# Causal convolution into a token-mixing MLP: one band matrix, halo rows in the loads, weights cast by their loads, and a written job list

## The chip, the cores and the metric

The kernel runs on one core of one Trainium2 chip. The metric is the device time of one execution in microseconds (us), as the median of several runs. Engines are named as the profile names them: PE (TensorE), PEld (its weight loads), DVE (VectorE), ACT (ScalarE), POOL (GpSimd) and SP (SyncE).

## The reference

The input x has 8 batches of 4224 tokens with 192 channels. A causal convolution of 7 taps, with softmaxed weights for each of 8 heads of 24 channels, gives y. Then an MLP mixes tokens through a 64-wide inner space.

```python
w = softmax(weight)                                  # 8 heads, 7 taps
y[b, s, h] = sum_k w[h, k] * x_pad[b, s + k, h]      # x_pad: 6 zero rows in front
wq, wk = y @ w_q, y @ w_k                            # 192 -> 64
W_tok = (wq @ wk.T) / sqrt(64)
out = relu(W_tok @ y) @ w_out                        # 192 -> 192
```

Since nothing nonlinear stands between the two products, W_tok @ y is wq @ (wk.T @ y), and wk.T @ y is w_k.T @ (y.T @ y). The kernel computes the small matrix G = y.T @ y once per batch.

## The kernel before

Everything is a list of operations for five engines, made by a planner in Python when the program is built. Each engine runs its list in order, and each operation waits on semaphores for what it needs. An engine whose next operation waits stands still, whatever is behind it.

**Tiling.** A batch has two halves of 2112 tokens, each cut into 18 chunks of 122 tokens. A chunk is loaded with the 6 rows ahead of it, so it fills 128 partitions; the last chunk has 38 tokens. `XW` holds five batches of x in bf16 (`NX = 5`).

**The stages of a batch.**

- Y (L512 for batch 0, L543 after): the convolution as a matmul with a band matrix for each head. All chunks use `BAND`; the last chunk of a half uses `BANDL`, so a head's last group takes two matmuls. The result goes from PSUM to `Y` (L955, ACT or DVE).
- D: copies 64 columns of `Y` beside the others, so that G can be made from 128-wide windows. For batches 2 and later it runs on POOL.
- T (L953): a transpose on DVE into `YB`. Q (L608): w_q times y, in four row groups and two column groups of PE, for each half of the chunks. It takes four PSUM banks.
- G (L637): six matmuls of 64 columns for each of 18 chunks, all into one PSUM bank. GEV copies G out, TR (L663, L664) transposes a part of it, MM (L677) multiplies by w_k, and the result lands in `M_SB`. No Z of a batch can start before all of its G.
- Z (L713): M times q, 13 jobs a batch, with a relu on the way out (L958 ACT, L959 DVE).
- O (L756, L758): z times w_out, 9 jobs a batch. The result goes to a ring of 8 buffers, `OUT` (`o_sb`), and from there to HBM by SP.

**Loads.** POOL issues the loads of x, which cast f32 to bf16 on the way. Batch 0 comes in eight groups in the order of use. Each further batch comes in two parts: `first` loads chunk 0 of the first half in two pieces without its six halo rows (those are zeroed once), `rows` loads the other chunks, `last` the short ones (L284). Batches 1 to 4 are issued at the start, and D of batch b issues batch b + 4. The loads of w_k and w_out go through SP in f32 into `WST`, and ten jobs W on ACT and DVE cast them. The cast of w_q is on ACT.

**The order.** The planner keeps streams of jobs (Q, W, GEV, TR and MM, O, Z, D, T, Y, G). At each step it takes the job that a model of the engines calls ready, and among several the one with the lowest key, a due time worked out from `KEYS`. It also puts dummy matmuls on PE (L966) where it expects PE to wait early in the run. The evacuation of each job goes to ACT or DVE, whichever the model has free first.

## Time and profile before

| | us |
|---|---|
| median of 13 runs | 161.24 (160.08 to 163.04) |
| the profiled execution | 161.61 |
| its span | 159.5 |
| PE busy in it | 144.1 |
| ACT busy | 129.0 |
| DVE busy | 116.5 |
| POOL busy | 62.2 |

The span is what the profile covers of one execution; the remaining 2.1 us of that execution lie outside it. Line numbers such as L543 are those of the kernel before. A helper records every evacuation, so all of them have L955, L958, L959, L960 or L961, and they are told apart by the tile that they write. Matmuls are pipelined and their ends are modelled, so the distance from one start to the next tells more than the duration of one; some matmul records are missing from the trace.

### The profile page before, as it was taken

To read this page: it belongs to the slowest core of one execution; us is meant where nothing else is said; L and a number is where in the kernel's file an instruction comes from. 1 tells how busy PE (TensorE), PEld (TensorE's weight loads), DVE (VectorE), ACT (ScalarE), POOL (GpSimd) and SP (SyncE) were. 2 spreads that over 40 slices of the span, in tenths; PEclk is the share of its full clock that TensorE was granted. 3 is DMA by queue.
4 is the path that set the end of the run, shared out by engine and by line. 5 is a ranking of instruction groups with operands and counts; after the bars stand their busy time and mean duration, and the time that the engine had idled before them with its cause. 6 is when DMAs were issued, how large, how long until landed. Compare 5 with 4: busy or idle time off the path is not lost.

```text
span 159.5 us, 5869 instructions
## 1 busy us (share of the span) xinstructions
PE 144.1 (90%) x2553; PEld 109.7 (69%) x2584; DVE 116.5 (73%) x233; ACT 129.0 (81%) x225; POOL 62.2 (39%) x83
## 2 busy tenths in 40 slices
PE   5898858999997999999999999999899999999930
PEld 4897753777775677766776787687667777776720
DVE  6758556998748788869778887997679839656700
ACT  8644638999876999799789887978698989799960
POOL 7999999899990755022002020202011020000000
PEclk9999999999999999999999999999999999999995
DMA  3999999999999999999999999999996454669997
GB/s 47 181 168 205 191 191 192 191 190 265 215 254 317 295 199 273 330 264 297 286 292 289 295 290 241 276 339 295 263 318 235 180 218 176 246 259 375 360 384 253
DMA packets 48281, 40.44 MB, mean 254 GB/s; under 512 B 38144, under 2 KB 40320, under 8 KB 48256
## 3 DMA queue, kind: packets, MB, share of 16 engines
q0 software_dynamic: 36784, 13.63, 71.9%
q1 hardware_dynamic: 11472, 26.45, 46.0%
q8 instruction: 20, 0.33, 0.8%
q14 instruction: 5, 0.04, 0.1%
HBM read 27.73 MB, written 25.95 MB: 337 GB/s over the span
## 4 chain that ended last, share of the span: by engine, by line
PE 75%; DMA 6%; ACT 5%; POOL 4%; issue 3%; DVE 3%; ACTq 0%; POOLq 0%
PE ps L637 16%; PE ps L756 13%; PE ps L543 12%; PE ps L758 12%; PE ps L608 9%; PE ps L713 9%; DMA xw<-in_x_dram 6%; POOL xw L268 3%; ACT y L955 2%; ACT o_sb L955 1%; DVE yb L953 1%; PE ps L677 1%; ACT qt L955 1%; DVE zt L959 1%; PE ps L966 1%
## 5 line engine op out<-in xcount | busy, mean ns | idle before, releaser
L955 ACT COPY o_sb<-ps 128x768 f32<-128x768 f32 (+1 forms) x63 | 47.2, 778 | 4.6 <-PE ps L758 3.4
L955 ACT CAST y<-ps 128x864 bf16<-128x864 f32 (+4 forms) x52 | 40.9, 812 | 6.5 <-PE ps L512 5.4
L756 PE MATMUL ps<-wo,zt 128*128 128x192 bf16 x256 | 42.6, 248 | 0.4 <-DVE m_sb L961 0.2
L758 PE MATMUL ps<-wo,zt 128*128 128x384 bf16 x128 | 41.7, 326 | 0.0
L268 POOL DMA_DIRECT2D xw<-in_x_dram x51 | 40.8, 816 | 1.5 <-POOLq L1101 0.8
L955 POOL COPY y<-y 128x1152 bf16<-128x1152 bf16 x12 | 13.9, 1156 | 67.4 <-ACT y L955 53.7
L637 PEld LDWEIGHTS ps<-y 128*128 128x128 bf16 x864 | 32.5, 98 | 8.4 <-ACT y L955 0.6
L637 PE MATMUL ps<-y 128*128 128x64 bf16 x864 | 35.8, 193 | 1.5 <-ACT y L955 0.4
L959 DVE TENSOR_SCALAR zt<-ps 128x512 bf16<-128x512 f32 x47 | 31.2, 683 | 8.0 <-PE ps L713 5.7
L953 DVE STREAM_TRANSPOSE yb<-y 128x576 int32<-128x576 int32 x48 | 33.6, 748 | 0.3 <-ACT y L955 0.2
L756 PEld LDWEIGHTS ps<-wo,zt 128*128 128x128 bf16 x256 | 25.5, 115 | 9.4 <-ACT o_sb L955 1.3
L543 PE MATMUL ps<-xw,band 128*128 128x432 bf16 (+1 forms) x112 | 28.5, 336 | 0.7 <-ACT m_sb L960 0.3
L958 ACT ACTIVATE zt<-ps 128x512 bf16<-128x512 f32 x49 | 28.7, 632 | 0.0
L955 DVE CAST y<-ps 128x864 bf16<-128x864 f32 (+2 forms) x20 | 19.3, 964 | 8.4 <-PE ps L543 5.4
L713 PE MATMUL ps<-qt,m_sb 128*128 128x512 bf16 x65 | 21.8, 380 | 0.3
L955 ACT CAST qt<-ps 128x576 bf16<-128x576 f32 (+2 forms) x21 | 11.7, 583 | 9.3 <-PE ps L608 9.3
L955 DVE CAST qt<-ps 128x234 bf16<-128x234 f32 (+1 forms) x27 | 10.3, 419 | 9.3 <-PE ps L608 9.3
L608 PE MATMUL ps<-yb,wq 32*64 32x288 bf16 x768 | 15.7, 284 | 1.5 <-issue 1.2
L543 PEld LDWEIGHTS ps<-xw,band 128*128 128x128 bf16 x112 | 9.8, 97 | 7.2 <-ACT m_sb L960 0.7
L758 PEld LDWEIGHTS ps<-wo,zt 128*128 128x128 bf16 x128 | 14.5, 113 | 0.0
L713 PEld LDWEIGHTS ps<-qt,m_sb 128*128 128x128 bf16 x96 | 8.8, 97 | 5.7 <-ACT y L955 0.9
L608 PEld LDWEIGHTS ps<-yb,wq 32*64 32x64 bf16 x768 | 10.5, 102 | 2.9 <-issue 1.9
(78 smaller groups left out, 117.0 us busy)
## 6 DMA issues: line engine op xcount, KB each, us to landing
out_dram<-o_sb SPq DMA_DIRECT2D x31, 768.0 KB, 7.3
xw<-in_x_dram POOLq DMA_DIRECT2D x21, 384.0 KB, 27.2
xw<-in_x_dram POOLq DMA_DIRECT2D x7, 432.0 KB, 26.4
xw<-in_x_dram POOLq DMA_DIRECT2D x4, 240.0 KB, 5.6
out_dram<-o_sb SPq DMA_DIRECT2D x16, 48.0 KB, 5.5
out_dram<-o_sb SPq DMA_DIRECT2D x2, 384.0 KB, 3.2
xw<-in_x_dram POOLq DMA_DIRECT2D x8, 42.0 KB, 13.5
xw<-in_x_dram POOLq DMA_DIRECT2D x1, 288.0 KB, 6.2
```

What stands on the lines that cost most here:

```text
L268: return e.dma_start(XW[lo:hi, b % NX, half, c : c + n, :], bass.AP(x_t, at, [[D, hi - lo], [CW * D, n], [1, D]]),)
L543: last = e.matmul(o.rearrange("p (c h d) -> p h c d", h=2, d=GRP), band_[:, h, :], rhs, start=True, stop=True, skip_group_check=True,)
L608: last = e.matmul(PS[64 * h : 64 * h + 64, bk + i, 0:288], WQ[r, j, :], rhs, start=j == 0, stop=j == 5, skip_group_check=True)
L637: last = e.matmul(PS[:, 7, 64 * k : 64 * k + 64], y[:, 64 * k : 64 * k + 128], y[:, 64 * k : 64 * k + 64], start=c + h + k == 0, stop=c == ...
L677: last = e.matmul(PS[:, bk, 64 * k : 64 * k + 64], WK[:, w], src, start=j == 0, stop=j > 2, skip_group_check=True)
L713: return e.matmul(PS[:, bk, :], m[:, parts[k] : parts[k] + 128], q, start=True, stop=True)
L756: e.matmul(o[:, 192 * h : 192 * h + 192], z[:, h, cols], WO1[:, :], start=h == 0, stop=False, **kw)
L758: last = e.matmul(o[:, 0:384], z[:, 2, cols], WO2[:, :], start=False, stop=True, **kw)
L953: return e.transpose(o, i)
L955: return e.copy(o, i) if eng == "act" else e.tensor_copy(o, i)
L958: return e.activation(o, i, AF.Relu)
L959: return e.tensor_scalar(o, i, 0.0, None, op0=ALU.max)
```

## The change

`BANDL` goes: all chunks use `BAND`, and G of the last chunk reads only its 38 valid rows. Batches 1 and later load chunk 0 together with the others, halo rows included, and a new job H zeroes the six rows on DVE once the load is there. Two groups of batch 0 come through SP in f32, into the idle `OUT` buffers, and are cast by ACT and DVE. w_k and w_out are loaded by POOL with the cast in the load, after batch 0; five small copies (the two jobs W) make the variants of the weights. The cast of w_q and two clears move to POOL. Batch 1 comes in four parts, batch 0 in fewer and wider Y jobs. D of batch b issues the load of batch b + 3, and D may go to DVE where POOL is late. The dummy matmuls get wider and fewer. The loop over keys is replaced by `ORDER`, a string with one letter for each job (E is GEV, M is TR and MM in turn, h sets banks aside for a coming Q); the model still decides who evacuates.

```diff
+ORDER = (
+    "YYDYYYDYDGDGGGYDGYYGDGTYTYDhYGhGTGDGGhGGHTGQYDGGWGTEMYMTYYYDZYZGGGTQYZGDGWGGDZZZ"
+    "YOZOOGGGGhGGZTTHGYQGGGYYGYZDEZTYYZGZMGTGDTYGTYZTMGGGGOGOOGGHZQTGGYZGOYZOZZGYDZGY"
+    "TGGZOZZOEYTTOGGYZGQGGYGTZDYZGHMhOGGZQYTGMTGYTTYOZOGOGZZGTZOYOOGZZOGZGDYGEQTGZZMG"
+    "GhQOGZGYYTZOOGHGZYTOGGZMDYGGGYGZGYYOZGZGOZZGDGEOTZQGZMZGGTOYYOGTOZYGDYZZGGhMOGGT"
+    "QHOGZGZTZOGZYOGGZZZYYZGOGYTTOTZOGZGhOEDQZGOYOGTGZTGGMYYOZOGGMZYZODGTOOGHZZGGYZOh"
+    "GGGYThQGZZGZQZTOGYGEZYOOZZZOMYDGYMGYGGZGTZOOTZZZGTGGTYDTGOGOGGQZZZGGOTTZTGZOQZGGO"
+    "QGOGOEMZZZOMOOZZZOZZZZOOOZZZOOZZZOZOOOO"
+)
...
-    BANDL = sbuf("bandl", [128, H, 128], BF16)
-    WST = sbuf("wst", [128, 4, D], F32)
-    WARM = sbuf("warm", [128, 128], BF16)
+    WARM = sbuf("warm", [128, 512], BF16)
...
+        ((0,), 6, 11, EIGHT), ((1,), 5, 10, EIGHT), ((0,), 11, 18, FOURS), ((1,), 10, 14, EIGHT),
         ((1,), 14, 18, FOURS),
-    ]] + [[((0, 1), 0, 9, PAIRS), ((0, 1), 9, 18, PAIRS)]] * (B - 1)
+    ], [
+        ((0,), 0, 9, FOURS), ((1,), 0, 9, FOURS), ((0,), 9, 18, FOURS), ((1,), 9, 18, FOURS),
+    ]] + [[((0, 1), 0, 9, PAIRS), ((0, 1), 9, 18, PAIRS)]] * (B - 2)
...
+    staged = [OUT[:, g, :, :].rearrange("p h c -> p (h c)")[:, 0 : 5 * D] for g in range(2)]
+    for g in range(2):
+        half, c, _, _ = GROUPS[0][g]
+        P.dma(
+            "sp",
...
+                bass.AP(x_t, at, [[D, 128], [CW * D, 5], [1, D]]),
+            ),
+            xg[0][g],
+        )
...
-    rows(0, 0, 1, 0, 128, 5, xg[0][0], ())
+    rows(0, 0, 6, 0, 128, 5, xg[0][3], ())
     bits = pool(lambda e: e.iota(BITS[:, :], [[1, H]], base=127, channel_multiplier=-1))
-    rows(0, 1, 0, 0, 128, 5, xg[0][1], ())
     first(0, xg[0][2], z_first)
-    rows(0, 0, 6, 0, 128, 5, xg[0][3], ())
     rows(0, 1, 5, 0, 128, 5, xg[0][4], ())
...
-    warm(16, [z_warm])
+    warm(4, [z_warm])
...
+    x_cast = act(lambda e: e.copy(fine[0], staged[0]), [xg[0][0]])
...
-    wqs = [act(lambda e: e.copy(WQ[:, :, :], WSQ[:, :, :]), [wl[0]])]
-
-    short = [dve(lambda e: e.tensor_copy(BANDL[0:64, :, 0:LAST], BAND[0:64, :, 0:LAST]),
-                 [*band, z_bandl])]
...
-        if part == 0:
-            first(b, xg[b][0], old)
-            rows(b, 0, 1, 0, 128, 8, xg[b][0], old)
-            rows(b, 1, 0, 0, 128, 9, xg[b][0], old)
+        if b == 1:
+            half, c = part % 2, 9 * (part // 2)
+            rows(b, half, c, 0, 128, 9 - part // 2, xg[b][part], old)
         else:
-            rows(b, 0, 9, 0, 128, 8, xg[b][1], old)
-            rows(b, 1, 9, 0, 128, 8, xg[b][1], old)
-            last(b, xg[b][1], old)
...
+            for half in range(2):
+                rows(b, half, 9 * part, 0, 128, 9 - part, xg[b][part], old)
+        if part == (2 if b == 1 else 1):
+            last(b, xg[b][part], old)
...
+    wload(WK[:, 0], wk_t, 0, DH, wl[1], 2)
+    wload(WK[:, 1], wk_t, 64, DH, wl[1], 2)
+    wload(WK[0:64, 2], wk_t, 128, DH, wl[1], 2)
+    wload(WK[64:128, 2], wk_t, 0, DH, wl[1], 2)
     load(1, 0)
     load(1, 1)
+    wq = [pool(lambda e: e.tensor_copy(WQ[:, :, :], WSQ[:, :, :]), [wl[0]], 0.55)]
+    z_wk = pool(lambda e: e.memset(WK[:, 3:6], 0.0))
+    load(1, 2)
+    z_m = pool(lambda e: e.memset(M_SB[:, :, :], 0.0), (), 0.85)
...
+    load(1, 3)
+    load(2, 0)
+    wload(WO1[:, :], wo_t, 0, D, wl[2])
+    wload(WO2S[0:64, :], wo_t, 128, D, wl[2])
+    wload(WO2S[64:128, :], wo_t, 128, D, wl[2])
+    z_wo2 = pool(lambda e: e.memset(WO2[:, :], 0.0))
+    load(2, 1)
...
-                for band_, a0, a1 in parts(c0, c1):
-                    rhs = XW[:, b % NX, :, a0:a1, GRP * h : GRP * h + GRP]
...
+                rhs = XW[:, b % NX, :, c0:c1, GRP * h : GRP * h + GRP]
+                last = e.matmul(
+                    PS[:, k + j, 0 : 48 * n].rearrange("p (c h d) -> p h c d", h=2, d=GRP),
+                    BAND[:, h, :], rhs, start=True, stop=True,
+                )
...
+    def job_halo(b):
+        return Job(
+            ("H", b), 0, None, [], groups=[xg[b][0]],
+            evacs=[(lambda bk: [(XW[0:6, b % NX, 0, 0, :], None)], ("H", b), 96, "zero")],
         )
...
-        if kind == "D" and job.name[1] > 0:
-            prefetch(job.name[1] + NX - 1, job.name[2])
...
+        if kind == "D" and job.name[1] > 1:
+            prefetch(job.name[1] + NX - 2, job.name[2])
...
+            if what == "zero":
+                eng = "dve"
...
+    for c in ORDER:
+        if c == "h":
+            bk = pick(4)[0]
+            hold[:] = range(bk, bk + 4)
+            continue
+        s = {"E": "GEV", "M": "MC"}.get(c, c)
+        job = streams[s][head[s]]
+        t = ready(job)
+        place(job, max(t, free["pe"]) if job.pe else t)
         head[s] += 1
```

## The prediction

> **What bounds the kernel now.** I read the page first: who is busy, and when the DMA is.

> ```profile
> span 159.5 us, 5869 instructions
> ...
> PE 144.1 (90%) x2553; PEld 109.7 (69%) x2584; DVE 116.5 (73%) x233; ACT 129.0 (81%) x225; POOL 62.2 (39%) x83
> ...
> GB/s 47 181 168 205 191 191 192 191 190 265 215 254 317 295 199 273 330 264 297 286 292 289 295 290 241 276 339 295 263 318 235 180 218 176 246 259 375 360 384 253
> ...
> q8 instruction: 20, 0.33, 0.8%
> ```

> PE is the busiest, but busy time includes modelled ends. DMA runs at about 190 GB/s from the second slice to the ninth: that is x alone, counted in the bf16 that it writes. Second, the windows by stage.

> ```profile
> 8.00:12.00 4.00, 4.00 (x85) 3.92 (x84) 2.35 (x7) 1.69 (x4) 4.00 (x6) 1.00 1.43 168
> 20.00:24.00 4.00, 2.38 (x74) 2.09 (x79) 2.19 (x4) 1.40 (x5) 3.65 (x7) 1.00 1.60 191
> 40.00:80.00 40.00, 38.38 (x707) 28.50 (x716) 31.06 (x60) 35.13 (x61) 17.44 (x20) 1.00 1.34 273
> 80.00:120.00 40.00, 39.02 (x707) 28.86 (x717) 32.80 (x58) 34.52 (x58) 5.43 (x5) 1.00 1.28 292
> 120.00:140.00 20.00, 19.47 (x393) 15.38 (x397) 14.54 (x26) 17.58 (x32) 1.47 (x2) 1.00 0.54 203
> ```

> The columns are PE, PEld, DVE, ACT, POOL, granted clock, DMA share, GB/s. From 40 us PE is nearly full, ACT at 87% and DVE at 80% are not; in the head PE is partly idle or does dummies (L966). Third, the chain of waits in the head.

> ```profile
> 7.65 8.90 DMA xw<-in_x_dram
> 16.60 0.51 PE ps L512 x8
> ...
> 19.33 0.48 ACT y L955
> 19.84 0.35 ACT wo L955
> 20.19 0.25 ACT wo2s L955
> 20.44 0.38 ACT y L955
> 20.93 0.86 PE ps L637 x24
> 21.79 1.18 issue
> ...
> 26.98 1.65 PE ps L713 x6
> ```

> The head ends with batch 0's last x at about 17 us, then Y, G, an unexplained PE stall, and the first Z at 26.98.

> **Work on PE.** From starts in the timeline: G 0.029 us a matmul, O 0.33 for 768 columns, Z 0.215, Q 0.95 with both changes of mode, Y 0.195 for a pair with `BANDL` and 0.1825 without a pair. One batch is 3.0 Y + 3.15 G + 1.9 Q + 2.65 Z + 5.4 O + 0.25 = 16.4; eight make 131.3. At 26.98 about 10.1 is done (Y, G, Q of batch 0, half of Y of batch 1), so 121.2 is left. The last matmul ends at 153.1, 126.1 later: the body loses 4.9 us. The tail is 6.4 (last evacuation, last store).

> **The change, part by part.**

> *Second band.* Rows:

> ```profile
> L543 PE MATMUL ps<-xw,band 128*128 128x384 bf16 x56 | 14.2, 326 | 0.1
> L543 PE MATMUL ps<-xw,bandl 128*128 128x48 bf16 x56 | 10.3, 184 | 0.0
> ```

> The 10.3 us is mostly overlap; by the starts each pair gives back 0.0125 us: 56 x 0.0125 = 0.7 us, and G on 38 rows still streams 64 columns. Worth 0.7.

> *Loads of batch 0.* Now x is 1.70 MB written at 0.185 MB/us = 9.2 us, plus 0.49 MB of weights at 0.38 (the rate of the last slices) = 1.3: 10.5 us from 3.2 to 13.7 in theory, 17.2 in fact. After: two groups are f32 through SP, 0.98 MB at 0.38 = 2.6; the rest 1.21 at 0.185 = 6.5; w_q 0.5: 9.6 us, and from 2.0, when SP's first data moves now. That is 2.1 us earlier, 3.1 if the 3.5 us of friction shrinks with it; I take 2.6: last x at 14.6. POOL issues eight loads in place of ten ahead of that, about 1.6 us less. The casts on ACT (0.85) and DVE (0.55) lie in the wait for later groups; without it they'd cost 0.5 on the first Y.

> [...]

> *From last x to the first Z*, now 9.8 us. The ten casts go: ACT's `wo` and `wo2s` (0.60) lay in the chain. In the string, 5.3 us of PE work lie from the last Y of batch 0 to Z, with 0.8 of waits for GEV, TR and MM. But half of batch 1's Y stands ahead of that Z. Its parts follow w_k (0.7) in the queue at 2.26, 2.26, 2.2 us each (432 and 417 KB at 0.19): 17.6, 19.9, 22.0, 24.0. So Z starts at about 22.5, with 9.2 us of work done, and 10.1 is reached at 23.4 where before it was 26.98: 3.6 us gained. POOL's memsets, the w_q cast and IDENT end at 16.8 by its row (0.87 a load), ahead of Q and TR.

> *w_out late.* It now stands behind batch 1 and half of batch 2 in POOL's queue: 24.0 + 4.6 + 0.5 = 29.1 if the queue is strictly in order, nearer 26 if small loads slip past. The letter W sits at 12.4 us of work (25.7), O at 13.8 (27.1). The W copies park ACT or DVE until it lands, with Z and Y evacuations behind them, and O waits: loss 0 to 2.5. I take 1.0.

> *Halo.* Seven loads of 10 rows go (0.53 us of POOL each, idle there). Seven memsets of 0.14 on DVE come, 1.0 us beside 20% idle: 0 on the path. Each waits for its load, though, and DVE's evacuations stand behind it.

> *Instruction stalls.* The chain has "issue" waits on PE of 1.18, 0.85, 0.37 and 0.32 us, with 20 fetches of 16 KB in q8. [...] The rows say 2.7 us for 20 fetches while x fills the DMA. The change takes out about 144 band instructions and many dummies, one or two fetches: 0.2. Where the rest fall shifts with the order: -1 to +1.2.

> *The order itself.* It can recover part of the 4.9, of which stalls are 2.4 and waits for evacuation the rest. A fixed order can lose as much where a landing differs. I take 0.3, from -2 to +2.

> *Later prefetch.* Costs nothing: loads wait long in the queue. The last one is issued at 61.42 and lands 58.9 us later, at 120.3.

> ```profile
> xw<-in_x_dram POOLq DMA_DIRECT2D x2, 384.0 KB, 55.4
> xw<-in_x_dram POOLq DMA_DIRECT2D x1, 432.0 KB, 57.6
> xw<-in_x_dram POOLq DMA_DIRECT2D x1, 33.0 KB, 58.9
> ```

> *Sum.* 130.6 in all, 10.1 done at 23.4: 120.5 left + 4.9 + 1.0 - 0.5 (order and stalls) gives the last matmul at 149.3; with 6.4, a span of 155.7. That is 3.8 under 159.5. The profiled execution took 161.61 for its 159.5; the median is 161.24, 1.74 over the span: **157.4 us**.

> **The rivals.**

> *x bounds it.* Batch 7's first part lands at 113.5 now (the row of 57.6 us), and its Y runs at 116.7: 3 us of slack. In the string that Y has 94.0 us of work ahead of it, so PE comes to it at 110 to 112. Stores share the DMA, so the lead of 2.6 us may not hold. If the part lands at 113.5 as now, 36.6 us of work at 96% and 6.4 follow: span 158.0, median 159.8. At the 2 us lead left after w_out: 156.0. For it: DMA share above 1.2 until 120. [...]

> *The order recovers the body.* w_out lands near 26, and 1.5 to 2 us of the 4.9 vanish: span 153.5, median 155.2. Against: ACT at 87% leaves little room.

> *Slower: the weights inside x's queue.* If batch 0 doesn't land earlier (staged f32 writes twice the bytes), w_out lands at last x + 14.5, and O waits for it and the copies. O's place (13.8 us of work) was reached at 30.8 before. With last x at 17.2, O starts at 32.1, 1.3 late, the band gives 0.7 back, and one blocked DVE evacuation or stall (0.5 to 1) adds: span 160.5 to 161, median 162.5. It decides from last x at about 16.6.

> **How the numbers follow.** The sum 0.55; x bound 0.22; recovered body 0.11; slower 0.12, of which a part ends near no change. About 0.3% (0.5 us) is what a measurement of this kernel can tell from no change. Faster 0.86, same 0.04, slower 0.10. The range leaves out the upper tenth and the best tenth: 154.2 to 160.6.

> **What would show it.** Right: L512 with the last group of batch 0 near 15 us, first Z near 22.5, first O before 29.5; no second L543 pair; last matmul near 149; last x near 118 to 120. Wrong: ACT or DVE parked at a WO2 copy or a halo memset over 1 us; PE waiting for `xw` after 60 us; last x of batch 0 after 16.6; more than 4 us of "issue".

## The result, and the profile after

The changed kernel takes 160.08 us (median of 11 runs, 159.74 to 160.62) where the kernel before took 161.38 in the runs beside it: a ratio of 0.9933, 95% interval 0.9905 to 0.9960. By that ratio it is faster by 1.1 us, where 3.8 were forecast; the ratio leaves out runs more than 1.5% above the fastest of their kernel, so it is not quite that of the medians. The profiled execution took 160.48 us for a span of 158.7.

First the page of the changed kernel, the lines that answer to those shown of before:

```profile
span 158.7 us, 5556 instructions
...
PE 141.3 (89%) x2400; PEld 102.6 (65%) x2428; DVE 119.2 (75%) x235; ACT 128.9 (81%) x216; POOL 59.8 (38%) x77
...
PEclk9999999789999999999999999999999999999996
...
GB/s 106 254 193 177 192 191 190 192 191 273 210 193 271 335 273 287 192 304 344 253 332 242 322 268 270 315 289 307 324 371 167 333 231 241 79 308 373 348 372 182
...
q8 instruction: 19, 0.31, 0.7%
```

PE's busy time fell by 2.8 us and the span by 0.8. One row is new: PEclk, the granted clock, which was 9 in every slice before the last in the kernel before, has a dip in the eighth and ninth slices, near 30 us. The row of the kernel before, for comparison:

```profile
PEclk9999999999999999999999999999999999999995
```

The windows of the changed kernel show where the dip lies:

```profile
8.00:12.00 4.00, 2.98 (x66) 2.62 (x66) 2.62 (x6) 2.01 (x4) 4.00 (x6) 1.00 1.57 193
20.00:24.00 4.00, 3.42 (x45) 2.61 (x47) 3.91 (x9) 3.50 (x7) 4.00 (x8) 1.00 1.60 191
28.00:30.00 2.00, 0.22 (x2) 0.25 (x3) 0.61 (x3) 0.66 (x2) 2.00 (x3) 0.95 1.59 192
30.00:32.00 2.00, 2.00 (x10) 1.25 (x9) 1.32 (x2) 1.74 (x4) 1.54 (x3) 0.50 1.61 191
32.00:34.00 2.00, 2.00 (x24) 1.55 (x23) 1.66 (x4) 1.26 (x3) 2.00 (x3) 0.70 1.60 193
40.00:80.00 40.00, 39.38 (x733) 29.68 (x739) 34.31 (x62) 37.22 (x65) 18.39 (x20) 1.00 1.36 267
80.00:120.00 40.00, 39.11 (x691) 28.90 (x701) 32.98 (x58) 36.14 (x61) 5.74 (x5) 1.00 1.25 304
120.00:140.00 20.00, 19.58 (x364) 14.68 (x368) 16.66 (x32) 17.80 (x30) 1.15 (x1) 1.00 0.59 216
```

The columns are those of the prediction's windows: PE, PEld, DVE, ACT, POOL, granted clock, DMA share, GB/s. Then the rows of the band and of the last piece of x, from the groups and from the DMA issues of 60 to 90 us (median us to landing at the end):

```profile
L539 PE MATMUL ps<-xw,band 128*128 128x432 bf16 x96 | 24.4, 347 | 0.1
```

```profile
xw<-in_x_dram POOLq DMA_DIRECT2D x1, 33.0 KB, 44.6
```

The pair is one matmul now, and the piece that took 58.9 us to land takes 44.6, since it is issued later. In the windows at 20 to 24 us PE, VectorE and ACT all do more than before: the head is ahead, as forecast. From 28 to 30 us PE does next to nothing, and then it is "busy" at half the clock. From 40 us on PE is 98% busy, a little fuller than before. The timeline of PE, and then of ACT, says what stood there (in brackets the idle time ahead of an instruction and what ended it):

```profile
23.31 0.39 PE L715 MATMUL ps<-qt,m_sb 128*128 128x512 bf16 x1
...
27.01 0.53 PE L505 MATMUL ps<-xw,band 128*128 128x216 bf16 x4
29.78 0.48 PE L758 MATMUL ps<-wo,zt 128*128 128x192 bf16 x2 [2.24 <-ACT wo L954]
30.05 0.53 PE L760 MATMUL ps<-wo,zt 128*128 128x384 bf16 x1
```

```profile
29.34 0.35 ACT L954 COPY wo<-wo2s 64x192 bf16<-64x192 bf16 x1 [2.72 <-DMA wo2s<-in_moe_w_out_dram]
```

The first Z starts at 23.31 us (26.98 before, 22.5 forecast), and the last x of batch 0 landed at 13.8 (17.2 before, 14.6 forecast). Then the first O waits 2.24 us for `WO2`, whose copies wait for w_out, landed at 29.3. After the wait an O matmul of 384 columns takes 0.53 us by its row where later rows say 0.33: the trace's clock record has PE at 0.5 for 3.41 us from 29.80. The chain of waits has the same place as one long piece:

```profile
20.24 0.56 POOL wo L347
20.80 0.53 POOL wo2s L347
21.33 7.93 DMA wo2s<-in_moe_w_out_dram
```

The last matmul ends at 151.7 us (153.1 before, 149.3 forecast) and the tail is 7.0 (6.4 before).

### The profile page after: what moved, and what is told of

It reads as the page before. It is cut to its first block, busy times and chain, and to the rows that moved or that the text cites. A ratio compares the mean times of both kernels' runs of the same rounds, so it can differ in the third digit from the quotient of the medians.

```text
span 158.7 us, 5556 instructions
## 1 busy us (share of the span) xinstructions
PE 141.3 (89%) x2400; PEld 102.6 (65%) x2428; DVE 119.2 (75%) x235; ACT 128.9 (81%) x216; POOL 59.8 (38%) x77
## 3 DMA queue, kind: packets, MB, share of 16 engines
q1 hardware_dynamic: 12032, 27.14, 47.7%
## 4 chain that ended last, share of the span: by engine, by line
PE 72%; POOL 12%; DMA 5%; ACT 3%; issue 3%; DVE 1%; ACTq 0%; POOLq 0%
PE ps L639 14%; PE ps L758 14%; PE ps L760 13%; PE ps L539 11%; PE ps L715 10%; PE ps L609 8%; POOL xw L275 7%; DMA wo2s<-in_moe_w_out_dram 5%; ACT o_sb L954 2%; POOL wk L347 2%; POOL xw L292 1%; PE ps L679 1%; DVE o_sb L954 1%; PE ps L752 1%; DVE qt L954 0%
## 5 line engine op out<-in xcount | busy, mean ns | idle before, releaser
L954 ACT CAST y<-ps 128x864 bf16<-128x864 f32 (+6 forms) x49 | 39.7, 838 | 5.7 <-PE ps L505 3.4
L639 PEld LDWEIGHTS ps<-y 128*128 128x128 bf16 (+1 forms) x864 | 35.5, 98 | 13.2 <-issue 2.9
L639 PE MATMUL ps<-y 128*128 128x64 bf16 (+1 forms) x864 | 40.1, 193 | 1.9 <-DVE y L954 1.1
L954 POOL COPY y<-y 128x1152 bf16<-128x1152 bf16 x12 | 13.8, 1147 | 64.3 <-ACT y L954 51.8
L758 PEld LDWEIGHTS ps<-wo,zt 128*128 128x128 bf16 x256 | 27.1, 115 | 12.8 <-ACT wo L954 2.5
L950 DVE STREAM_TRANSPOSE yb<-y 128x576 int32<-128x576 int32 x48 | 35.2, 756 | 0.1
L275 POOL DMA_DIRECT2D xw<-in_x_dram x35 | 32.2, 932 | 2.0 <-POOL xw L434 1.1
L957 ACT ACTIVATE zt<-ps 128x512 bf16<-128x512 f32 x50 | 29.1, 611 | 0.9 <-PE ps L760 0.5
L539 PE MATMUL ps<-xw,band 128*128 128x432 bf16 x96 | 24.4, 347 | 0.1
L954 DVE CAST qt<-ps 128x288 bf16<-128x288 f32 (+1 forms) x30 | 11.6, 425 | 9.9 <-PE ps L609 9.9
L954 ACT CAST qt<-ps 128x576 bf16<-128x576 f32 (+1 forms) x18 | 10.8, 610 | 5.9 <-PE ps L609 5.5
L760 PEld LDWEIGHTS ps<-wo,zt 128*128 128x128 bf16 x128 | 14.7, 115 | 0.0
L609 PEld LDWEIGHTS ps<-yb,wq 32*64 32x64 bf16 x768 | 10.5, 102 | 2.6 <-issue 0.7
L505 PE MATMUL ps<-xw,band 128*128 128x120 bf16 (+4 forms) x96 | 8.5, 226 | 2.0 <-DVE xw L954 0.8
## 6 DMA issues: line engine op xcount, KB each, us to landing
xw<-in_x_dram POOLq DMA_DIRECT2D x14, 432.0 KB, 16.5
xw<-in_x_dram POOLq DMA_DIRECT2D x14, 384.0 KB, 24.4
out_dram<-o_sb SPq DMA_DIRECT2D x2, 384.0 KB, 3.9
```

Source lines behind the costliest of these rows:

```text
L275: return e.dma_start(XW[lo:hi, b % NX, half, c : c + n, :], bass.AP(x_t, at, [[D, hi - lo], [CW * D, n], [1, D]]),)
L505: last = e.matmul(PS[:, bk + j // per, at : at + w], BAND[:, h, :], XW[:, b % NX, half, c0:c1, GRP * h : GRP * h + GRP], start=True, stop= ...
L539: last = e.matmul(PS[:, k + j, 0 : 48 * n].rearrange("p (c h d) -> p h c d", h=2, d=GRP), BAND[:, h, :], rhs, start=True, stop=True,)
L609: last = e.matmul(PS[64 * h : 64 * h + 64, bk + i, 0:288], WQ[r, j, :], rhs, start=j == 0, stop=j == 5, skip_group_check=True)
L639: last = e.matmul(PS[:, 7, 64 * k : 64 * k + 64], y[:, 64 * k : 64 * k + 128], y[:, 64 * k : 64 * k + 64], start=c + h + k == 0, stop=c == ...
L758: e.matmul(o[:, 192 * h : 192 * h + 192], z[:, h, cols], WO1[:, :], start=h == 0, stop=False, **kw)
```

## The experiments

Most of these kernels have the same instruction order on PE, ACT and VectorE as the changed one, so one VectorE instruction can serve as a milestone in all of them: the 7th, the 10th and the 46th of its 48 StreamTransposes. From the 7th to the 10th is the piece with the wait for w_out, from the 10th to the 46th is the body. The table is read from the profiled executions; the experiments refer to it.

| kernel | us, median | 7th to 10th | 10th to 46th |
|---|---|---|---|
| the changed kernel | 160.08 | 15.04 | 93.75 |
| w_out early | 160.54 | 11.46 | 97.78 |
| w_out early, half the stores | 156.16 | 11.46 | 93.88 |
| w_out late, half the stores | 159.81 | 15.51 | 93.75 |
| shifted by 120 instructions | 163.65 | 13.60 | 97.87 |
| w_out early, late halos on GpSimd | 159.82 | 11.90 | 96.96 |
| w_out early, stores held back, let go late | 161.81 | 11.48 | 94.08 |
| w_out early, stores held back, let go earlier | 157.90 | 11.46 | 94.04 |

**w_out early.** The three w_out loads go one place forward in POOL's queue.

```diff
+    wload(WO1[:, :], wo_t, 0, D, wl[2])
+    wload(WO2S[0:64, :], wo_t, 128, D, wl[2])
+    wload(WO2S[64:128, :], wo_t, 128, D, wl[2])
     load(2, 0)
-    wload(WO1[:, :], wo_t, 0, D, wl[2])
...
```

> The changed kernel with one move: POOL issues the three loads of w_out ahead of batch 2's first part, not behind it. Theory 1 (late w_out: PE stood 2.2 us ahead of the first O, and then ran some 4 us at half the granted clock): w_out lands near 25, no wait ahead of the first O, granted clock 1.00 from 28 to 36 us, and 3.5 to 4 us off the changed kernel's time, about 156.3. Theory 2 (the last x bounds the end: it landed at 123.4 and its Y ran at 123.5): the head is as early as theory 1 says, but PE then waits for x of batch 7, and the time falls by 0 to 1 us, to 159.1 or more.

Measured: 160.54 us, ratio 0.9940 (0.9910 to 0.9971), not told apart from the changed kernel. w_out landed at 24.6, the wait and the half clock are gone, and the 10th transpose comes 3.6 us sooner by the table. The body then loses 4.0. The timelines of VectorE and of PE:

```profile
94.39 0.14 DVE L952 MEMSET xw<- 6x96 uint32 x1 [3.20 <-DMA xw<-in_x_dram]
94.46 0.62 DVE L958 TENSOR_SCALAR zt<-ps 128x512 bf16<-128x512 f32 x1
```

```profile
95.13 0.54 PE L539 MATMUL ps<-xw,band 128*128 128x432 bf16 x2 [2.08 <-DVE zt L958]
95.51 0.48 PE L758 MATMUL ps<-wo,zt 128*128 128x192 bf16 x2
```

x of batch 6 is not there when VectorE comes to its halo; the relu queued behind the clear holds PE's banks, PE stands 2.08 us, and again the clock is 0.5, from 95.55 for 3.41 us. So a first cause is seen, and a second one behind it: a PE that is ahead runs into x.

**Dummies in the gap.** 24 dummy matmuls ahead of the first O of the changed kernel.

```diff
+            if job.name == ("O", 0, 0, 0):
+                k = min((k for k in range(7) if k not in held and k not in hold),
+                        key=lambda k: banks[k][0])
+                fill(k, 24, banks[k][1])
```

> The changed kernel with w_out as late as it is, but 24 dummy matmuls of 256 columns (some 2.6 us at full clock) on PE in the wait ahead of the first O. Theory 1: the wait stays, the granted clock stays at 1.00 from 28 to 36 us, and about 1.9 us of the 4 comes back: near 158.2. If the clock is worth nothing at the end because x bounds it (theory 2): 159.5 to 160.1.

Measured: 162.80, ratio 1.0104 (1.0062 to 1.0146): a miss. The bank that the dummies took was itself emptied by ACT, behind the parked copy, so they started at 30.03, after the wait, and added their own 4.15 us. It says nothing on what the clock alone costs. One thing in it counts: with the stores 2.9 us later than in the changed kernel, the last x of batch 7 landed at 115.8 in place of 123.4.

**w_out early, short pieces first.** As the first, and `last()` issued ahead of `rows()`.

```diff
-        if part == (2 if b == 1 else 1):
-            last(b, xg[b][part], old)
...
+        if part == (2 if b == 1 else 1):
+            last(b, xg[b][part], old)
         if b == 1:
```

> As the kernel with w_out early, and in each batch's last part the short chunks (33 KB, 44 rows) are issued ahead of the long ones, not behind. In the changed kernel the long loads of batch 7 had landed at 116.8 and the short one 6.6 us later, with x at 7 to 16 KB/us. Theory 2: the last x lands several us earlier (117 to 119) and the time falls below that of the kernel with w_out early by up to 3 us. Theory 1: no difference between the two (within 0.4 us).

Measured: 160.67, ratio 0.9966 (0.9929 to 1.0004). Nothing won; the last x still landed at 122.6, VectorE stood up to 3.6 us at a halo clear and PE 2.49 us behind it at 114 us, with half the clock after it. Which piece comes last does not matter, since all of x is late.

**Half the stores, with w_out early and late.** Each large store writes 64 partitions in place of 128, so half of those output rows are left out.

```diff
-                parts = [(at, [[4 * D, 128], [HALF * D, 2], [1, 4 * D]], OUT[:, orr, :, :])]
+                parts = [(at, [[4 * D, 64], [HALF * D, 2], [1, 4 * D]], OUT[0:64, orr, :, :])]
```

> As the kernel with w_out early, but each large store writes only 64 of its 128 partitions, so half of the output is left out (all matmuls and evacuations stay). Theory x (x and stores take turns on the DMA engines one descriptor at a time, 384 against 3072 bytes; the stores hold x back, and PE, once it is ahead, waits for x of batches 6 and 7 and then runs at half clock): x of batch 7 lands well before 115, no wait for x after 30 us, and the time falls to 154 to 156. Theory order (the written order costs its 4 us in waits between engines, whatever x does): within 1 us of the kernel with w_out early, 159.5 to 160.5.

> The changed kernel as it is (w_out's copies late), with each large store writing 64 partitions in place of 128; half of those output rows are never written. It is the fourth corner of a square: w_out late or early, stores whole or half (160.08, 160.54 and 156.16 us are known). If the late w_out costs the head some 4 us that nothing later gives back, and x was only just in time in the changed kernel, halving the stores brings little: 159.2 to 160.3, with the wait for wo2s and the half clock at 30 to 34 us unchanged. If the stores' traffic holds the changed kernel back by itself (x late in its second half), it falls towards the other half-store kernel: 156 to 157.5. In between would mean that each takes a part.

Measured: early 156.16, ratio 0.9656 (0.9594 to 0.9719); late 159.81, ratio 0.9855 (0.9796 to 0.9914). By the medians the square reads: late and whole 160.08, early and whole 160.54, late and half 159.81, early and half 156.16. Either step alone moves the median by half a microsecond or less; both together by 3.9. (By the ratios, 0.9855 and 0.9933, the late kernel with half the stores is 1.3 us faster than the changed one, and the intervals just touch; its body is the same 93.75 in the table, and its tail is 0.8 us shorter, 6.2 for 7.0.) So the late w_out costs 3.6 us that come back only if x is in time, and x costs 4.0 us only if w_out is not late. With half the stores and w_out early, x of batch 7 landed at 93.8, and no engine waited for x after 30 us.

**Half the stores in the kernel before.** The same edit there.

> The kernel before with the same halved large stores (half of those output rows are never written). If the kernel before is bound by its engines and by what starts them, not by the DMA queues, it stays at 160.5 to 161.5 (less up to 1 us in the tail, where the last large store is shorter). If x against the stores already bounds it, as it does the kernel with w_out early, it gains as much as that one did, some 4 us: 157 to 158.

Measured: 162.09, ratio 1.0018 (0.9973 to 1.0062). Less traffic brought the kernel before nothing (0.4 us at most by the interval), so the DMA queues did not hold it back; x stayed ahead of PE there, and in its profile no engine waited for x after 20 us.

**Smaller store packets.** w_out early; each large store as two of 384 KB, issued one after each O job, with pieces of 1536 B in place of 3072.

```diff
+        cut = not rem
...
-            if tail:
+            if cut:
                 return [(
                     OUT[:, orr, q, :].rearrange("p (h r d) -> p r h d", h=2, r=2),
...
-            elif tail:
+            else:
                 parts = [(at + 2 * q * D, [[4 * D, 128], [HALF * D, 2], [1, 2 * D]],
...
-            else:
-                parts = [(at, [[4 * D, 128], [HALF * D, 2], [1, 4 * D]], OUT[:, orr, :, :])]
```

> As the kernel with w_out early, but every large store goes out in two halves, one after each O job, with descriptors of 1536 bytes for 3072; same bytes, same order on all compute engines. Theory x: beside a store x moves at about 60 KB/us in place of 38, so batches 6 and 7 land earlier, the waits for x at 90 to 120 us go, and the time falls by 3 to 4 us, to 156 to 157. Theory order, or DMA full whatever the shares: 159.5 to 160.5.

Measured: 168.55; the runs scatter from 164.96 to 169.38 (168.91 for the profiled one), so no ratio is given. A store packet of 1536 B takes 78 ns, one of 3072 B 134. The stores last longer: for the same 27.14 MB the packets of their queue took 50.9% of 16 engines' span of 167.1 us, 85 us, where with w_out early they took 47.3% of 159.0, 75 us. And what the queues carry together falls. That can be put in one unit: alone, x moves 190 KB a us (as bf16) and stores 385 (the tail). From 36 to 112 us x/190 + stores/385 is 0.98 in the changed kernel, 0.98 with w_out early, 0.93 here and 0.81 with half the stores. I read 0.98 as full DMA engines. But the kernel before stands at 0.98 as well and gained nothing from half the stores: in these runs full DMA engines cost time only where PE came to x before x had landed.

**Halo clears off VectorE.** w_out early; all clears on GpSimd, and then those of batches 3 to 7 only (the edit shown).

```diff
-            ev = P.op(eng, f, waits)
+            late = what == "zero" and key[1] > 2
+            if late:
+                waits = waits + [o for o in P.ops["pool"] if o.dma is None][-1:]
+            ev = P.op("pool" if late else eng, f, waits)
```

> As the kernel with w_out early, but the seven halo clears are done by POOL, not DVE; the rest of each engine's list is as it was. There DVE stood 3.2 us at the clear of batch 6. Theory x: PE comes to the Y of that batch and waits there itself; 0 to 1 us is gained. Theory halo (the clear parks DVE, and PE starves for evacuations that would have been possible): 3 us or more is gained, near 157.

> The kernel with w_out's loads early (160.54 us), the halo clears of batches 3 to 7 on GpSimd in place of VectorE, so that VectorE no longer stands at a clear while x is on its way. If what costs is x itself being late, PE still waits for batch 6 near 94 us and the time stays at 160.0 to 161.2. If VectorE parked at the clear, with the relu and the copies queued behind it, is what costs, it falls by the 2 us that PE stood there and the slow clock after it: 157.5 to 158.8. GpSimd then stands at the clears instead, and the issues of later loads behind it: where that decides, it is slower, 161.5 to 163.

Measured: all on GpSimd 175.65, ratio 1.0857 (1.0794 to 1.0921): batch 1's clear stood behind GpSimd's issues of the initial loads and PE waited 17.0 us for it, so the experiment missed its question. Batches 3 to 7 only: 159.82, ratio 0.9875 (0.9825 to 0.9926), 0.7 us less than with the clears on VectorE by the medians (the intervals of the ratios overlap), and the body still loses 3.2 of the 4.0 us. GpSimd then stands 21.2 us at the clears in three waits, the longest 10.8. A parked VectorE is the smaller part; x being late is the larger.

**One band in the kernel before.** The pair `BAND`, `BANDL` becomes one matmul over all the chunks; G of the last chunk reads 38 rows; order and all else as before.

```diff
-                for band_, a0, a1 in parts(c0, c1):
+                for band_, a0, a1 in [(BAND, c0, c1)]:
...
-                y = Y[:, b % 2, c, h, :]
+                y = Y[0 : 128 if c < NCK - 1 else LAST, b % 2, c, h, :]
```

> The kernel before, with its order and all else as it was, but without the second band's matmuls: one matmul a head and group, G of the last chunk on 38 rows. The prediction's step: 56 pairs at 0.0125 us and 16 narrow ones, 0.7 us less (ratio 0.996). Rival: the freed PE time is spent in waits for evacuation, 0.2 us or less.

Measured: 166.04, ratio 1.0312 (1.0274 to 1.0351): slower by 5 us where 0.7 less was expected. PE has less to do and does it in more time. The weight loads' waits and PE's own:

```profile
PEld ps L543 <- issue: 2.1, 3, 1.7
PEld ps L756 <- issue: 2.1, 6, 0.9
...
PEld ps L637 <- issue: 1.5, 2, 1.2
PEld ps L608 <- issue: 1.5, 3, 1.0
```

```profile
PE ps L608 <- issue: 1.9, 2, 1.2
...
PE ps L637 <- issue: 1.0, 1, 1.0
```

"Issue" is a wait for nothing that the profile shows. Ahead of PE's matmuls it sums to 3.7 us here and to 2.4 in the kernel before; ahead of weight loads it sums to 8.0, but not all of that is lost: the changed kernel has 8.8 there and only 0.5 ahead of its matmuls. If it is the loading of instructions, it depends on where in the order one loaded block ends.

The traces on record speak for it. The queue of instruction loads (q8 on the page) moves 20 pieces of 16 KB for this kernel's 4995 matmuls and weight loads on its page, some 250 each; in the kernel before it is 20 for 5137 (257 each), in the changed kernel 19 for 4828 (254 each). These pieces are the blocks meant below. In all twenty traces of this study, PE stood at "issue" for 0.3 us or more fourteen times, and each time the stand ended 1.26 to 1.54 us after the end of such a piece, though the pieces start some 3 to 13 us apart. More than this the traces do not show of it.

**The same, shifted.** 80 narrow dummies in place of 20 at the start: 60 more matmuls, each with its weight load, so 120 more PE instructions.

```diff
-    warm(20, [])
+    def warm_short(e):
+        for _ in range(80):
+            o = e.matmul(PS[:, 0, 0:32], WARM[:, :], WARM[:, 0:32], start=True, stop=True)
+        return o
+
+    P.op("pe", warm_short, [])
```

> The kernel before without the second band, as run, with 80 short dummy matmuls in place of 20 longer ones on the idle PE at the start, 120 PE instructions more ahead of all real work, at the same time on PE. That kernel took 166.0 with PE waits on nothing visible (issue) in seven places. Theory fetch (what decides is where the blocks of 256 PE instructions end, since a fetch waits in the full DMA): the shift moves the stalls, and the time changes by 2 us or more, back towards 161. Rival (the missing matmuls themselves upset the order between engines): no change, 165.5 to 166.5.

Measured: 161.00, ratio 0.9992 (0.9979 to 1.0005). 120 added instructions take 5 us off. "Issue" ahead of matmuls sums to 0.4 us in place of 3.7, and the longest is 0.2 in place of 1.2; that is 3.4 of the 4.7 us between the spans (163.7 and 159.0). Without the second band and so shifted, the kernel gains less than 0.4 us on the kernel before, though it has 2.0 us less of "issue" on PE; what the band is worth by itself stays open.

**The changed kernel, shifted.** The same 120 instructions more at its start.

```diff
-    warm(6, [])
+    def warm_short(e):
+        for _ in range(66):
+            o = e.matmul(PS[:, 0, 0:32], WARM[:, 0:128], WARM[:, 0:32], start=True, stop=True)
+        return o
+
+    P.op("pe", warm_short, [])
```

> The changed kernel, same order, with the second set of six wide start-up matmuls replaced by 66 narrow ones: 120 instructions more on PE before the first useful one, so that the borders of its 256-instruction blocks fall elsewhere in the order. If fetching the blocks stalls PE wherever a border meets a stretch of short matmuls, and the written order was found for the old borders, it is slower by 1 to 5 us (161 to 165) with PE standing at 'issue' in more places than before. If the borders don't matter for this order (its worst stretches were spread), 159.7 to 160.5.

Measured: 163.65 (162.18 to 166.24), ratio 1.0104 (1.0057 to 1.0150), 2.8 us more than the changed kernel by the ratios. The profiled execution is the fastest of them, 162.18. PE stands at "issue" for 4.2 us in place of 0.5: the windows show it standing for one stretch of two microseconds, and the timeline a second stall of 1.2.

```profile
72.00:74.00 2.00, 2.00 (x67) 1.51 (x63) 1.62 (x4) 1.52 (x4) 0.00 (x0) 1.00 1.14 341
74.00:76.00 2.00, 0.03 (x1) 0.00 (x0) 0.00 (x0) 0.78 (x1) 0.00 (x0) 1.00 1.13 340
```

```profile
60.21 0.43 PE L614 MATMUL ps<-yb,wq 32*64 32x288 bf16 x10 [1.20 <-issue]
```

By the table its body lost 4.1 us; the two stalls are 3.7 of them. It also shows the clock apart from the wait: PE waited 2.0 us for w_out here too, but the clock stayed at 1.00, and the piece from the 7th to the 10th took 13.60 in place of 15.04. So of the 3.6 us that the late w_out cost in the traced execution, 2.1 are the wait and 1.4 the half clock. Not every execution need have that half clock, or pay for it in full at the end: of the changed kernel's twelve executions on record (the median leaves one out), six with a mean granted clock of 0.989 or more took 159.69 to 159.94 us, six with 0.984 or less 160.08 to 160.62. Only one of the twelve was traced, so what the dip is worth over the whole kernel stays open.

**Stores held back.** Open was whether there is too much to move or only in the wrong order. w_out early; each store of batches 1 to 5 is issued four stores late, by `LAG = 4` (then five; then four with the late halos on GpSimd). Nothing is left out. `issue` is what issues a store:

```diff
+            held_back.append(issue)
+            while len(held_back) > (LAG if 0 < b < B - 2 else 0):
+                held_back.pop(0)(evs)
```

> The kernel with w_out early (160.54 us), each store of batches 1 to 5 issued four stores later than its data is there, all of them let go at batch 6; nothing left out, PE, ACT, VectorE and GpSimd orders unchanged. If x is late only because stores are ahead of it, some three large stores (2.3 MB, 6 us at the 370 to 390 GB/s of the tail) move behind x: x of batch 6 is there before 90 us, of batch 7 before 116 us, the 4 us come back, 156.3 to 157.5, and the tail stays near 7 us since the queues are half idle from 124 to 144 us. If the DMA engines simply have too much to move, the held stores are lacking at the end and the tail grows by what x gains: 159.5 to 160.8. If the output's slots run out, ACT and VectorE wait for stores: 161 or more.

> As the other, but five stores back in batches 1 to 5, two back in batch 6, none in batch 7. If order alone decides and the last x still meets the burst at batch 6 in the other kernel, this one is the better by up to 1 us: 156.0 to 157.3. If five places are too many for the eight output slots, copies into o_sb wait for a store to land (waits of ACT or VectorE on o_sb's DMA) and it is slower than the other by 1 to 3 us. If the total of traffic decides, 159.5 to 161.

> Stores held back by four as in the first, and the halo clears of batches 3 to 7 on GpSimd. If x is in time everywhere, no engine stands at a clear for long, and moving the clears off VectorE (5 x 0.14 us busy) brings 0 to 0.4 us: 156.0 to 157.5. If x is still late, it shows the 0.7 us that this move brought to the kernel with w_out early and no held stores.

Measured: four places 161.81, ratio 1.0013 (0.9983 to 1.0044); five 166.15, ratio 1.0279 (1.0225 to 1.0332); four with halos on GpSimd 162.02, ratio 1.0030 (1.0000 to 1.0061). With four, x of batch 7 landed at 105.6, PE waited for no x, and the last matmul ended at 149.1. But the tail was 11.7 us. The windows of four places, to be read for the last number, GB/s:

```profile
112.00:120.00 8.00, 7.79 (x171) 5.36 (x170) 6.15 (x11) 7.16 (x13) 1.15 (x1) 1.00 0.46 163
120.00:128.00 8.00, 7.95 (x118) 6.21 (x118) 7.91 (x16) 7.73 (x14) 1.15 (x1) 1.00 0.69 267
128.00:136.00 8.00, 7.68 (x219) 5.72 (x218) 5.85 (x12) 6.63 (x12) 0.00 (x0) 1.00 0.45 160
136.00:144.00 8.00, 7.83 (x67) 5.60 (x70) 5.81 (x15) 7.60 (x12) 0.00 (x0) 1.00 1.03 388
```

The stores could have gone from 112 us on, and were still held: the first store of batch 6, which lets them go, came at 134.7. With five places the eight output slots ran out, and ACT and VectorE waited for a store to land:

```profile
ACT o_sb L963 <- DMA out_dram<-o_sb: 4.0, 3, 2.7
DVE o_sb L963 <- DMA out_dram<-o_sb: 3.1, 1, 3.1
```

**Stores let go earlier.** Against the edit above, the hold ends with batch 4: four places, three places, and four then two in batch 5.

```diff
-            while len(held_back) > (LAG if 0 < b < B - 2 else 0):
+            while len(held_back) > (LAG if 0 < b < B - 3 else 0):
```

> Stores of batches 1 to 4 held back by four, all let go at batch 5's first output (near 105 us, when x of batch 7 has landed), nothing else changed. If the order against x is all that costs, the backlog of some 2.4 MB drains from 106 to 130 us at 380 KB/us, the last matmul stays at 149.1 and the tail falls back to about 7: span 156, 157.0 to 158.0 us. If the DMA engines have too much to move in all, the tail keeps 9 to 12 us: 159.5 to 161.8.

> The same with stores held back by three. x of batch 6 and 7 lands some 1 to 2 us later than with four. If there was slack left at four (no engine waited for x there), the same 157.0 to 158.0; if three are too few, PE waits for x near 94 or 118 us by 1 to 2 us, with a stretch of half clock after a long wait: 158 to 160.

> Held back by four in batches 1 to 4, by two in batch 5, by none from batch 6. If x of batch 7 still needs the DMA while batch 5 is written, this is better than letting all go at batch 5; otherwise its tail keeps half of what the first kernel of this kind lost there, 2 to 2.5 us: 159 to 160.

Measured: 157.90, ratio 0.9813 (0.9756 to 0.9869); 157.88, ratio 0.9788 (0.9743 to 0.9833); in steps 158.60, ratio 0.9842 (0.9793 to 0.9890). The windows and the end of PE's timeline, four places:

```profile
104.00:112.00 8.00, 8.00 (x109) 5.76 (x108) 6.16 (x13) 7.81 (x14) 1.15 (x1) 1.00 0.92 348
112.00:120.00 8.00, 8.00 (x159) 5.41 (x159) 6.20 (x11) 7.17 (x13) 1.15 (x1) 1.00 0.34 122
120.00:128.00 8.00, 8.00 (x162) 6.29 (x160) 7.50 (x14) 7.53 (x13) 1.15 (x1) 1.00 1.02 385
128.00:136.00 8.00, 7.03 (x179) 4.83 (x164) 5.34 (x11) 5.70 (x11) 0.00 (x0) 1.00 0.92 337
```

```profile
148.96 0.33 PE L760 MATMUL ps<-wo,zt 128*128 128x384 bf16 x1
```

x of batch 7 landed at 108.4, and batch 5's first store came at 119.2, not at the 105 expected. The backlog then drains at 385 and 337 GB/s in the two windows from 120 to 136 us, the last matmul ends at 149.3 and the span at 156.1, a tail of 6.8. The same bytes in another order give back what x had cost: the order against x decided, not the total. PE still stood once at "issue", 0.97 us at 133 us; with the stores held to batch 6 the same order and the same blocks had no such stand there, with the DMA queues half idle (160 GB/s). The versions with four and with three places are faster than both kernels of the study: their intervals lie below that of the changed kernel (0.9905 to 0.9960).

## Why the prediction was wrong

*w_out late: the step that failed.* "Loss 0 to 2.5. I take 1.0." It measured 3.6 (15.04 less 11.46 in the table). The landing was the late end of the forecast, 29.3 for 29.1, so the small loads did not slip past x (the first of the three landed 0.7 us ahead of the last x issued before it); the sign that the forecast had named was there, ACT and VectorE parked at a `WO2` copy for 2.72 and 2.41 us; PE's wait was 2.24; what the sum did not have at all is the clock, 1.4 us. In the traces half speed lasted 3.41 us each time that it followed a wait of 2 to 5.4 us (in six kernels), and the full-speed stretch ahead of it in the changed kernel is 23.89, seven times as long. A wait of 2.08 us (w_out early) or 2.24 was enough (the last section has the border). The forecast did not ask what a wait does to the clock, though the change puts a DMA wait ahead of PE.

*The sum assumed that x follows.* Taking w_out's wait away did not bring the 157.4, since "loads wait long in the queue" was read as slack. x of batch 7 landed at 123.35 in the changed kernel, 0.18 us ahead of its matmul. The rival "x bounds it" (0.22) ends at 159.8, and that this lies next to the measured 160.08 is luck: with half the stores x of batch 7 landed at 92.6 and the changed kernel still took 159.81. The limit that it named is that of the kernel with w_out early; what it lacked is that a PE that is ahead sends its stores earlier, and from 36 to 112 us, at 0.98 of what the queues can carry by the unit above, a store moved forward is paid for with x. So the two costs stood one behind the other, and the sum had 1.0 us for both.

*The sum, term by term.* The last matmul was 2.4 late (151.7 for 149.3): 2.6 from w_out, 0.8 from the later first Z, and, by difference, 1.0 less lost in the body than taken. The tail was 0.6 longer, 7.0 for 6.4, with stores at 348 to 373 GB/s in the three slices from 143 to 155 us. Together 3.0, the difference of the spans (158.7 and 155.7).

*Second band, -0.7.* Not borne out: +5 us alone, and with the blocks shifted 0.9992, less than 0.4 us of gain; its worth apart from the blocks is not shown. A G matmul on 38 rows starts 29 ns after the one before it, as on 128 rows, so G gained nothing. *Instruction stalls, -0.2 (-1 to +1.2).* In the changed kernel "issue" on PE fell from 2.4 us to 0.5, more than was taken, and the range was too narrow: 120 instructions moved the kernel with one band by 5 us and the changed kernel by 2.8. With this one shift the explicit order lost 2.8 us, more than the whole change gained; whether it was found for its own blocks is not shown.

*Right:* batch 0's loads (13.8 for 14.6); the parts of batch 1 (17.3, 19.7, 22.0, 24.0 for 17.6, 19.9, 22.0, 24.0); no time for the halo on PE in the changed kernel, where VectorE's one wait at a clear was 0.7 us, at batch 1. The casts of the two f32 groups took 0.99 us on ACT and 0.66 on VectorE (0.85 and 0.55 taken), and x was 0.8 us ahead of its forecast beside them; no run took the casts away. The rival "weights inside x's queue" fell with the landing at 13.8.

## To carry to other kernels

When a head becomes faster, ask which transfer the gain runs into: put the DMA's load into one unit (each queue's bytes over its rate alone), and where it is at 0.98, as here, expect a store that is issued earlier to make a load later (stores 2.9 us later let the last x land 7.6 us sooner), which costs once PE comes to that load first; hold such stores back until the last load has landed, but no longer. A DMA wait of two microseconds ahead of PE cost some 1.4 us more in half clock here, so price it as both. A reordered program can also move the places where PE stands at "issue" (120 dummy instructions in front took 5 us off one kernel here and added 2.8 to another): test an order with some 100 of them in front before trusting a difference of a few per cent.
